# Score products of two heads at once: products over 64 rows in the two halves of the array, decay as bfloat16 rows

## Chip, core and metric

The kernel runs on one core of a Trainium2 chip. TensorE multiplies matrices into PSUM (8 banks), VectorE (DVE), ScalarE (ACT) and GpSimd (POOL) work on tiles in SBUF, SyncE (SP) issues most DMAs. The metric is the device time of one execution in microseconds. An instruction of TensorE takes a stationary operand (the weights, a load of its own in the trace: PEld) and streams a moving one through it, column by column. The array has 128 rows and 128 columns; a product can also occupy half of the rows or half of the columns.

## What is computed

Attention with decay for 4 x 8 heads, 576 positions, head size 64, then two feed-forward stages:

```python
scores = scale * np.matmul(q, k.transpose(0, 1, 3, 2))
cum = np.cumsum(np.log(np.clip(f, 0.0001, 1.0)), axis=-1)
decay = cum[:, :, :, None] - cum[:, :, None, :]
scores = np.where(causal, -1000000000.0, scores + decay)
scores = scores - np.max(scores, axis=-1, keepdims=True)
attn = np.exp(scores)
attn = attn / (np.sum(attn, axis=-1, keepdims=True) + 1e-09)
x = np.matmul(attn, v)          # then [2304, 512]
h = x @ w_in; x = (h / (1 + np.exp(-h))) @ w_out
y = ((x @ w_a) * (x @ w_b)) @ w_out2
```

## The kernel before

Heads are worked on in 16 pairs. A pair's 576 query rows are cut into five blocks (`IB`): four of 128 rows and one of 64. Block 0 needs 128 key columns, block 1 256, block 2 384, block 3 512; block 4 (64 rows of each head, both heads in one tile of 128 partitions) needs 576, in two parts of 288. For each pair, `load_pair` brings q and k, `score` multiplies block by block into PSUM banks named s, takes the row maxima on DVE (into p) and the exponentials on ACT; `inverse` transposes the sums (rs), and spreads their inverses over partitions by a DMA to DRAM and back (invs, rb); `attend` transposes the exponentials on TensorE (t_x, t_y), copies them to th, multiplies by v (pv, in fp32, the two heads in the two column halves of the array), scales by rb on DVE (xf) and writes x in two parts, on ACT and POOL.

Products are made in fp32r, whose operands are rounded, from a high and a low part: high by high, high by low and low by high. Before, this goes into two products over all 128 rows of the array. For each head there is a tile `side` of four slots of 576 columns. In the head's own half of the partitions stand the high parts; the other half holds the low parts, and in slots 2 and 3 a copy of a high part and the decay rows (cum in two parts, and constants). The line `a[:, 0] x a[:, 1]` (L564) gives high by high plus low by high, `a[:, 2] x a[:, 3]` (L566) the rest with the decay. To fill a side, `load_parts` has POOL load q and k with rounding into the head's half (L506), SP copy two slots between or within halves (L508), DVE or POOL subtract the high part from the raw q and k (L511), and SP load the decay rows twice (L516). There are four sides, so two pairs can be prepared at a time. Only pair 0 is different: its heads have tiles `whole` of 66 rows and one product in fp32.

What runs when is decided before the build by `Plan.order`: every piece of work has an engine, a duration, a priority and the buffers that it takes; a simple model of the engines places them in time, and the instructions are issued in that order on each engine. `Tag` stands for a rotating buffer; `SLOTS` has their numbers (before: s 2, t 2, pv 2, mm 2, eight banks in all). The first feed-forward chunk of the first two batches (`first_chunk`, ps and po, 128x288 products) is placed between the attention's work, the decoding of its weights (`plan_decode`) too. After the attention the rest of the feed-forward follows, which is products over 464 columns on TensorE to the end.

At the start `prepare` computes cum on 32 partitions (one for each head), writes its parts to DRAM (dec), and runs 66 idle products; `keep_warm` puts further idle products into TensorE's gaps in the first 40 us of the plan.

Of the kernel before, what the change touches and what calls it, by code (L numbers as in the profile page):

```python
# [55 lines left out]
class Tag:  # L56
# [31 lines left out]
class Plan:  # L88
# [44 lines left out]
    def order(self):  # L133
# [9 lines left out]
        while ready:  # L143
            cands = []
            for op in ready:
                t = 0
                for b in op.bufs:
# [3 lines left out]
                    f = b.tag.free_at() if b.tag.bufs[b.tag.next] is b else None  # L151
# [69 lines left out]
def model_kernel(ctx: ExitStack, tc: tile.TileContext, qk, v, f, w, out):  # L221
# [13 lines left out]
    dec = dram.tile([NH, 2, S], F32, name="dec")  # L235
# [6 lines left out]
    rows_sb = dp.tile([NH, 2, S], F32R, name="rows")  # L242
# [137 lines left out]
    ATT = ("s1", "qkr", "vt", "th", "t3", "t4", "xf", "p", "q", "nm", "sm", "rt", "rb")  # L380
# [14 lines left out]
    def prepare():  # L395
# [16 lines left out]
        def run_up():  # L412
            for n in range(RUN_UP):
# [11 lines left out]
        plan.add("DVE", 369, lambda: nc.vector.tensor_copy(rows_sb[:, 0], cum), ["cum"], [("rows", 0)], pr)  # L425
        plan.add("DVE", 669, lambda: nc.vector.tensor_sub(rows_sb[:, 1], cum, rows_sb[:, 0].bitcast(F32)),
                 ["cum", ("rows", 0)], [("rows", 1)], pr)
        plan.dma(480, 147000, lambda: nc.scalar.dma_start(dec, rows_sb.bitcast(F32)), rows_keys, ["dec"], pr, eng="ACT")
# [4 lines left out]


    sides = [sb.tile([P, 4, S], F32R, name=f"side{n}") for n in range(SLOTS["s1"])]

    def side(h):
        n = len(tags["s1"].bufs) % SLOTS["s1"]
        return Buf(tags["s1"], lambda: sides[n])

    def fill_sides():
        t = sides[-1]
        for n, to in enumerate(sides):
            plan.add("DVE", t_dve(2 * S), lambda to=to, n=n: nc.vector.tensor_scalar(
                half(to, 1 - n % 2)[:, 2:], ident[half_of(1 - n % 2), 0:1].unsqueeze(2).to_broadcast([D, 2, S]), 0.0, None, ALU.mult),
                [("const", 1)], [("side", n)], -7.5 + n)
        for r, i, value in ((4, 3, 1 / SCALE), (2, 2, -1 / SCALE)):
# [5 lines left out]
    def half_of(n):  # L453
        return slice(n * D, (n + 1) * D)

    def half(t, n):
        return t[n * D:(n + 1) * D]
# [450 lines left out]
```

## Time and profile before

| | us |
|---|---|
| three runs | 1088.75, 1089.15, 1089.7 |
| median | 1089.15 |
| profiled execution | 1086.86 |
| its span in the trace | 1085.2 |

The span is the time from the first to the last instruction in the trace; the profiled execution has 1.7 us around it, and is 2.3 us below the median. Durations in the trace are those of one instruction from its start to its modelled end; a stream of products overlaps, so what one adds to a stream is the distance from its start to the next one's start (its pitch).

### The profile page before, as it was taken

How to read it: one execution, taken by the hardware profiler on the slowest of the kernel's cores; microseconds unless marked ns; L12 is line 12 of the kernel's file. 1: busy time of each engine (PE TensorE's matmuls, PEld its weight loads, DVE VectorE, ACT ScalarE, POOL GpSimd, SP SyncE). 2: the span in 40 equal slices, each digit the busy share in tenths (PEclk: the TensorE clock that was granted, in tenths of full speed). 3: DMA queues.
4: the chain of work that ended last, by engine and by line, in shares of the span. 5: the costliest groups of instructions: out<-in, count | busy, mean ns of one | idle time of the engine just before them, and what ended most of it. 6: DMA issues, size and time to landing. Idle time of an engine off the chain costs nothing.

```text
span 1085.2 us, 16074 instructions
## 1 busy us (share of the span) xinstructions
PE 1051.2 (97%) x5625; PEld 914.0 (84%) x5625; DVE 675.7 (62%) x1562; ACT 435.2 (40%) x1082; POOL 354.3 (33%) x416
## 2 busy tenths in 40 slices
PE   8978999999999999999999999999999999999998
PEld 6756677778888889889889898988988988989987
DVE  5778566655998784774845976357366375473323
ACT  3667677775534432332323544343132132231110
POOL 5356445423533330421303774033042051240000
PEclk7989999999999999999999999999999999999999
DMA  5667667732212120110200112012011021010012
GB/s 133 173 187 183 166 173 186 173 94 69 71 58 77 50 78 1 59 59 1 79 1 20 59 43 84 30 40 79 1 59 59 1 78 40 17 62 1 18 53 105
DMA packets 40840, 79.14 MB, mean 73 GB/s; under 512 B 8036, under 2 KB 11252, under 8 KB 40760
## 3 DMA queue, kind: packets, MB, share of 16 engines
q1 hardware_dynamic: 38312, 69.13, 22.0%
q0 software_dynamic: 2400, 8.85, 3.6%
q8 instruction: 44, 0.72, 0.3%
q14 instruction: 36, 0.29, 0.1%
q10 hardware_dynamic: 48, 0.15, 0.0%
HBM read 64.25 MB, written 4.94 MB: 64 GB/s over the span
## 4 chain that ended last, share of the span: by engine, by line
PE 85%; DMA 5%; DVE 4%; ACT 2%; issue 1%; POOL 1%; SPq 1%; DVEq 0%; POOLq 0%; ACTq 0%
PE ps L301 15%; PE ps L302 15%; PE ps L303 15%; PE po L301 10%; PE po L302 10%; PE po L303 10%; PE pv L681 3%; DMA rb<-invs 2%; PE t_x L637 1%; DVE side L511 1%; PE s L564 1%; PE s L562 1%; DVE p L586 1%; PE t_y L637 1%; PE s L566 1%
## 5 line engine op out<-in xcount | busy, mean ns | idle before, releaser
L301 PE MATMUL ps<-x,whi 128*128 128x464 f32 (+1 forms) x760 | 282.6, 372 | 1.7 <-ACT acc L785 1.7
L302 PE MATMUL ps<-x,whi 128*128 128x464 f32 (+1 forms) x760 | 282.6, 372 | 0.0
L303 PE MATMUL ps<-x,wlo 128*128 128x464 f32 (+1 forms) x760 | 282.5, 372 | 0.0
L271 POOL TENSOR_TENSOR d<-d,whi 128x256 f32<-128x256 f32 x124 | 105.7, 860 | 431.3 <-ACT whi L270 431.0
L302 PE MATMUL po<-glo,whi 128*128 128x464 f32 (+1 forms) x520 | 192.4, 370 | 0.0
L303 PE MATMUL po<-ghi,wlo 128*128 128x464 f32 (+1 forms) x520 | 191.9, 369 | 0.0
L301 PE MATMUL po<-ghi,whi 128*128 128x464 f32 (+1 forms) x520 | 190.6, 371 | 0.0
L301 PEld LDWEIGHTS ps<-x,whi 128*128 128x128 f32 x760 | 142.5, 187 | 18.9 <-ACT acc L785 1.9
L303 PEld LDWEIGHTS ps<-x,wlo 128*128 128x128 f32 x760 | 142.4, 187 | 17.2
L302 PEld LDWEIGHTS ps<-x,whi 128*128 128x128 f32 x760 | 142.5, 187 | 17.0
L333 ACT CAST ghi<-g 128x464 fp32r<-128x464 f32 (+1 forms) x130 | 75.0, 577 | 153.5 <-DVE g L332 92.9
L272 POOL TENSOR_TENSOR wlo<-d,d 128x256 fp32r<-128x256 f32 x124 | 100.2, 816 | 35.9 <-DVE d L269 34.6
L263 ACT ACTIVATE d<-d 128x256 f32<-128x256 f32 x124 | 52.9, 433 | 145.6 <-DMA d<-in_w 136.8
L334 DVE TENSOR_TENSOR glo<-g,ghi 128x464 fp32r<-128x464 f32 (+1 forms) x130 | 90.7, 698 | 29.7 <-ACT ghi L333 29.2
L332 DVE TENSOR_TENSOR g<-g,ps 128x464 f32<-128x464 f32 (+1 forms) x60 | 37.8, 631 | 113.3 <-PE ps L303 113.3
L301 PEld LDWEIGHTS po<-ghi,whi 128*128 128x128 f32 x520 | 97.6, 188 | 10.8 <-PE po L303 0.2
L303 PEld LDWEIGHTS po<-ghi,wlo 128*128 128x128 f32 x520 | 97.6, 188 | 10.8
L302 PEld LDWEIGHTS po<-glo,whi 128*128 128x128 f32 x520 | 97.6, 188 | 10.3
L264 DVE TENSOR_SCALAR d<-d 128x256 uint32<-128x256 uint32 x124 | 44.9, 365 | 79.5 <-ACT d L263 78.7
L355 DVE SCALAR_TENSOR_TENSOR acc<-po,acc 128x464 f32<-128x464 f32 (+3 forms) x144 | 75.1, 549 | 26.6 <-PE po L303 26.6
L364 DVE TENSOR_TENSOR acc<-po,acc 128x464 f32<-128x464 f32 (+2 forms) x120 | 63.9, 552 | 26.1 <-PE po L303 25.3
L595 ACT ACTIVATE p<-p,nm 128x512 f32<-128x512 f32 (+3 forms) x128 | 70.8, 557 | 12.4 <-DVE nm L586 12.0
(118 smaller groups left out, 1507.2 us busy)
## 6 DMA issues: line engine op xcount, KB each, us to landing
d<-in_w SPq DMA_DIRECT2D x128, 256.0 KB
side<-in_qk POOLq DMA_DIRECT2D x30, 288.0 KB, 4.9
qk<-in_qk SPq DMA_DIRECT2D x15, 576.0 KB
side<-side SPq DMA_DIRECT2D x60, 144.0 KB
vt<-in_v SPq DMA_DIRECT2D x16, 320.0 KB
rb<-invs SPq DMA_DIRECT2D x32, 128.0 KB
out_t<-acc SPq DMA_DIRECT2D x12, 232.0 KB
d2ghi<-in_w SPq DMA_DIRECT2D x8, 256.0 KB
```

What stands on the lines that cost most here:

```text
L263: nc.scalar.activation(m, high.bitcast(F32), AF.Copy, scale=2.0 ** -112)
L264: nc.vector.tensor_scalar(m.bitcast(U32), m.bitcast(U32), 3, None, ALU.logical_shift_left)
L271: nc.gpsimd.tensor_sub(m, val, hi.bitcast(F32))
L272: nc.gpsimd.tensor_add(lo, m, e)
L301: nc.tensor.matmul(ps, wh, mh, start=start, stop=False)
L302: nc.tensor.matmul(ps, wh, ml, start=False, stop=False)
L303: nc.tensor.matmul(ps, wl, mh, start=False, stop=stop)
L333: nc.scalar.copy(ghi[:, t, :n], g)
L334: nc.vector.tensor_sub(glo[:, t, :n], g, ghi[:, t, :n].bitcast(F32))
L355: nc.vector.scalar_tensor_tensor(a, ps, 0.5, a, ALU.mult, ALU.add)
L364: nc.vector.tensor_add(a, ps, a)
L595: plan.add("ACT", t_act(sum(IB[ib]), 279), lambda b=b, c=c, nj=sum(IB[ib]): nc.scalar.activation(b()[:, :nj], b()[:, :nj], AF.Exp, bias=nm ...
```

## The change

The sides, the loads on POOL's queue, the copies and the subtractions by halves are gone. A pair has one raw tile of q and k (head 0 in partitions 0 to 63, head 1 in 64 to 127, as the array in DRAM has them), one cast of it to the high part (ACT, 128x1152), one subtraction for the low part (POOL or DVE, 128x1152), and a tile `decay` in bfloat16. cum is now in three bfloat16 parts that add up to it exactly; six rows (three parts and constants) stand at partitions 0 and 64 of the decay tile, zeros in the other rows.

A block's scores are four products over 64 rows for each head: decay (bfloat16), high by high, high by low, low by high. The two heads' products alternate; head 0's take rows 0 to 63 of the array, head 1's rows 64 to 127, into two banks. Block 4 has for each of its two parts the decay product and one product in fp32 from the raw tile; its heads use rows and columns 0 to 63, and rows and columns 64 to 127, and write the two halves of one bank. Blocks 1 and 0 form one group (256 and 128 columns in the same two banks).

The buffers change (s 3, pv 1, p 4, vt 2, xf 2, qkr 2), and the planner can place a piece of work that takes two buffers of one kind.

```diff
-    def free_at(self):
+    def free_at(self, ahead=0):
...
-        if len(self.old) < self.slots:
+        n = len(self.old) + ahead - self.slots
+        if n < 0:
             return 0
-        ops = self.old[0].ops
+        ops = self.old[n].ops
...
-    SLOTS = dict(s1=4, qkr=1, vt=1, th=4, t3=1, t4=1, xf=1, s=2, t=2, pv=2, mm=2, g=6, ghi=2, glo=2)
-    SLOTS.update(wh=2, p=3, q=6, nm=2, sm=2, rt=1, rb=1)
+    SLOTS = dict(qkh=2, qkl=2, dt=2, qkr=2, vt=2, th=4, t3=1, t4=1, xf=2, s=3, t=2, pv=1, mm=2, g=6, ghi=2, glo=2)
+    SLOTS.update(wh=2, p=4, q=6, nm=2, sm=2, rt=1, rb=1)
...
-        plan.dma(480, 147000, lambda: nc.scalar.dma_start(dec, rows_sb.bitcast(F32)), rows_keys, ["dec"], pr, eng="ACT")
+        for i, value in enumerate((-1 / SCALE, 1 / SCALE)):
+            plan.add("POOL", 1200, lambda i=i, value=value: nc.gpsimd.memset(rows_sb[:, 3 - 3 * i:6 - 3 * i, i], value), (), [("rows", "const", i)], -8)
+        rest = (ft, one)
+        for n in range(3):
+            src = cum if n == 0 else rest[n - 1]
+            plan.add("DVE", 450, lambda n=n, src=src: nc.vector.tensor_copy(rows_sb[:, n, 0], src), [("c", n), "cum"], [("rows", n)], -8)
+            if n < 2:
+                plan.add("DVE", 750, lambda n=n, src=src: nc.vector.tensor_sub(rest[n], src, rows_sb[:, n, 0]),
+                         [("c", n), ("rows", n), "cum"], [("c", n + 1), ("f", "one")[n]], -8)
...
-            plan.swdge(1040, 8 * D * S, lambda near=near, src=src: nc.gpsimd.dma_start(near()[:, 0:2], src), ["go"], [(s1, "h")], pr + p)
...
+        plan.dma(480, 16 * D * S, lambda: nc.sync.dma_start(raw(), qk[pair]), ["go"], [raw], pr)
         for p in range(2):
...
+            plan.dma(480, 0, lambda p=p: nc.sync.dma_start(dt()[p * D:p * D + 6], dec[2 * pair + p]), ["dec", ("decay", n)], [(dt, p)], pr)
+        plan.add("ACT", t_act(2 * S, 93), lambda: nc.scalar.copy(hi(), raw()), [raw], [(hi, "h")], pr)
+        (e1, d1, f1), two = ((e, d, lambda eng=eng: eng.tensor_sub(lo(), raw(), hi().bitcast(F32)))
+                             for e, d, eng in (("POOL", t_pool(2 * S), nc.gpsimd), ("DVE", t_dve(2 * S) + 300, nc.vector)))
...
+            steps = (4,) if whole else (0, 4) if shared else range(4)
+            todo = [(p, part, n) for part in range(2 if shared else 1) for n in steps for p in range(2)]
...
+                    elif step == 0:
+                        a = half(t["dt"](), p)
+                        nc.tensor.matmul(out, a[:, 0, i], a[:, 1, j], start=True, stop=False)
+                    elif shared:
+                        a = half(t["raw"](), p)
+                        nc.tensor.matmul(out, a[:, 0, i], a[:, 1, j], start=False, stop=True)
+                    else:
+                        a, b = ((t["hi"], t["hi"]), (t["hi"], t["lo"]), (t["lo"], t["hi"]))[step - 1]
+                        nc.tensor.matmul(out, half(a(), p)[:, 0, i], half(b(), p)[:, 1, j], start=False, stop=step == 3)
...
-    GROUPS = ((None, 4),), ((0, 3), (1, 3)), ((0, 2), (1, 2)), ((0, 1), (1, 1)), ((0, 0), (1, 0))
+    GROUPS = (4,), (3,), (2,), (1, 0)
```

The planner places everything anew. On TensorE, before, around the product with v of pair 4 (pv_4; a name is the tile, the pair, and for s the head or None, the block and the part; L757 to L759 are the feed-forward chunk, t_5 transposes):

```order
L637 MATMUL t_5_x0_1308<-ident_58,p_5_1_3_1273 128x2x64
L564 MATMUL s_5_0_0_0_1322<-side0_92 128x128
L681 MATMUL pv_4_1_1327<-th_4_0_1180,vt_4_1116 64x448 x2
L681 MATMUL pv_4_1_1327<-th_4_1_1220,vt_4_1116 64x448 x2
L681 MATMUL pv_4_1_1327<-th_4_2_1229,vt_4_1116 64x320 x2
L681 MATMUL pv_4_1_1327<-th_4_3_1242,vt_4_1116 64x192 x2
L681 MATMUL pv_4_1_1327<-th_4_4_1251,vt_4_1116 64x64 x2
L681 MATMUL pv_4_0_1357<-th_4_2_1229,vt_4_1116 64x128 x2
L637 MATMUL t_5_x1_1362<-ident_58,p_5_None_4_1244 128x128
L566 MATMUL s_5_0_0_0_1322<-side0_92 128x128
L637 MATMUL t_5_x2_1365<-ident_58,p_5_None_4_1244 128x128
```

The single products of a block stand between transposes and pv. After, at the same place (s is now named by pair, block and bank):

```order
L546 MATMUL s_5_1_0_1341<-qkh_5_1024,qkl_5_1034 128x128
L546 MATMUL s_5_1_1_1343<-qkh_5_1024,qkl_5_1034 128x128
L666 MATMUL pv_4_1_1367<-th_4_0_1257,vt_4_1067 64x448 x2
...
L666 MATMUL pv_4_1_1367<-th_4_4_1303,vt_4_1067 64x64 x2
L540 LDWEIGHTS decay1_93
L540 MATMUL s_6_4_0_1395<-decay1_93 64x288
L540 LDWEIGHTS decay1_93
L540 MATMUL s_6_4_0_1395<-decay1_93 64x288
L543 MATMUL s_6_4_0_1395<-qk_6_1057 64x288 x2
...
L543 MATMUL s_6_4_1_1400<-qk_6_1057 64x288 x2
L666 MATMUL pv_4_0_1413<-th_4_2_1277,vt_4_1067 64x128 x2
L622 MATMUL t_5_x0_1421<-ident_58,p_5_None_4_1234 128x128
```

Blocks 1 and 0 of pair 5 come as one run of products before pv_4_1, and block 4 of pair 6 stands between pv_4_1 and pv_4_0, which now use one bank in turn. On SP, before, the DMAs around the broadcast rb of pair 7:

```order
L508 DMA side0_92<-side0_92 64x576 x2
L508 DMA side1_93<-side1_93 64x576 x2
L499 DMA qk_10_1816<-in_qk 128x1152
L610 DMA invs_66<-rt_7_1851 9x128
L616 DMA rb_7_1896<-invs_66 64x512
L494 DMA vt_8_1910<-in_v 128x640
L618 DMA rb_7_1896<-invs_66 64x64
L616 DMA rb_7_1896<-invs_66 64x512
L618 DMA rb_7_1896<-invs_66 64x64
L516 DMA side3_95<-dec_65 2x576 x2
L516 DMA side2_94<-dec_65 2x576 x2
L508 DMA side2_94<-side2_94 64x576 x2
```

After, a pair's whole share of SP's queue (here around rb of pair 4; every later pair reads alike):

```order
L496 DMA decay1_93<-dec_65 6x1152 x2
L494 DMA qk_7_1232<-in_qk 128x1152
L485 DMA vt_5_1242<-in_v 128x640
L595 DMA invs_66<-rt_4_1282 9x128
L601 DMA rb_4_1336<-invs_66 64x512
L603 DMA rb_4_1336<-invs_66 64x64
L601 DMA rb_4_1336<-invs_66 64x512
L603 DMA rb_4_1336<-invs_66 64x64
```

The copies between halves and the dec loads by slots are gone from between the rb DMAs; two decay loads for each pair remain.

## Rows read from the trace of the kernel before

**Rows 1.** The page: busy time, share of the span and instructions of each engine.

```profile
PE 1051.2 (97%) x5625; PEld 914.0 (84%) x5625; DVE 675.7 (62%) x1562; ACT 435.2 (40%) x1082; POOL 354.3 (33%) x416
```

**Rows 2.** Busy time in four stretches: us, engines (instructions), granted clock, DMA share, GB/s.

```profile
40.00:120.00 80.00, 64.47 (x447) 47.26 (x446) 62.19 (x187) 55.68 (x169) 43.12 (x50) 0.94 0.73 181
120.00:200.00 80.00, 73.90 (x523) 57.89 (x523) 50.02 (x168) 57.35 (x168) 40.38 (x40) 0.98 0.69 169
200.00:260.00 60.00, 58.77 (x442) 47.71 (x439) 31.61 (x110) 42.30 (x127) 18.38 (x21) 1.00 0.43 117
...
300.00:400.00 100.00, 100.00 (x478) 89.47 (x478) 85.14 (x184) 39.21 (x87) 38.94 (x48) 1.00 0.20 64
```

**Rows 3.** The chain of work, 0 to 300 us: shares; then start, us, what.

```profile
by line: PE pv L681 12.1%; DMA rb<-invs 8.5%; issue 5.3%; PE t_x L637 4.4%; DVE side L511 3.1%; PE s L564 3.1%; PE s L562 2.9%; DVE p L586 2.9%; PE t_y L637 2.8%; PE s L566 2.5%; ACT p L595 2.1%; DMA side<-in_qk 2.0%; DMA d<-in_w 1.9%; DMA 
...
103.56 6.67 DMA rb<-invs
...
135.07 2.40 DMA rb<-invs
...
159.95 6.05 DMA side<-in_qk
```

**Rows 4.** The subtractions into the sides (L511) in stretches: DVE, POOL busy us.

```profile
220.00:240.00 20.00, 1.83 (x1) 1.38 (x1) 1.00 0.31 91
```

**Rows 5.** Groups by line and shape, 0 to 260 us: busy us, mean ns; idle time before.

```profile
L511 POOL TENSOR_TENSOR side<-qk,side 64x576 fp32r<-64x576 f32 x32 | 49.3, 1541 | 40.8 <-DMA qk<-in_qk 26.7 <-DMA side<-in_qk 10.6 <-DMA side<-dec 1.6
L511 DVE TENSOR_TENSOR side<-qk,side 64x576 fp32r<-64x576 f32 x28 | 31.9, 1139 | 7.0 <-DMA side<-in_qk 4.2 <-DMA qk<-in_qk 2.2
...
L681 PE MATMUL pv<-th,vt 128*64 128x448 f32 x128 | 28.4, 565 | 0.4 <-ACT x L692 0.4
...
L692 ACT CAST x<-xf 128x448 fp32r<-128x448 f32 x16 | 9.0, 564 | 10.6 <-DVE xf L689 10.2 <-POOL d1glo L721 0.5
...
L692 ACT CAST x<-xf 128x128 fp32r<-128x128 f32 x16 | 4.7, 296 | 0.4
```

**Rows 6.** DMAs, 0 to 260 us: the sum; issues by line, KB each, us to landing.

```profile
DMA packets 19188, 40.70 MB, mean 157 GB/s; under 512 B 5636, under 2 KB 5780, under 8 KB 19160
...
side<-in_qk POOLq DMA_DIRECT2D x30, 288.0 KB, 4.9
...
side<-side SPq DMA_DIRECT2D x60, 144.0 KB
```

**Rows 7.** TensorE in order of time, 107.3 to 108.6 us: start, us, line, what.

```profile
107.33 0.39 PE L566 MATMUL s<-side 128*128 128x512 f32 x1
107.56 0.71 PE L637 MATMUL t_y<-ident,p 128*128 128x128 f32 x5
108.05 0.44 PE L564 MATMUL s<-side 128*128 128x384 f32 x1
108.33 0.34 PE L566 MATMUL s<-side 128*128 128x384 f32 x1
108.50 0.38 PE L637 MATMUL t_y<-ident,p 128*128 128x128 f32 x2
```

**Rows 8.** TensorE in order of time: a pair's pv, and what follows it.

```profile
99.89 3.22 PE L681 MATMUL pv<-th,vt 128*64 128x448 f32 x24
103.04 0.33 PE L637 MATMUL t_x<-ident,p_None 128*128 128x128 f32 x1
```

**Rows 9.** TensorE in order of time, 130.2 to 130.6 us: into pv.

```profile
130.24 0.29 PE L564 MATMUL s_None<-side 128*64 128x288 f32 x1
130.37 0.29 PE L566 MATMUL s_None<-side 128*64 128x288 f32 x1
130.59 3.22 PE L681 MATMUL pv<-th,vt 128*64 128x448 f32 x24
```

**Rows 10.** The start, POOL and SP in order of time.

```profile
1.80 1.17 POOL L483 MEMSET whole<- 4x576 f32 x2
...
7.34 2.49 SPq L486 DMA_DIRECT2D whole<-cum  x4
```

More of the change, by code (lines that the diff above doesn't have):

```diff
@@ new lines, in prepare @@
+        rest = (ft, one)
[5 more added lines that the diff above has]
+                         [("c", n), ("rows", n), "cum"], [("c", n + 1), ("f", "one")[n]], -8)
+        plan.add("POOL", 2000, lambda: nc.gpsimd.tensor_copy(rows_sb[:, 3:, 1], rows_sb[:, :3, 0]),
+                 [("rows", n) for n in range(3)], [("rows", "k")], -8)
@@ L430, in model_kernel @@
+        plan.dma(480, 442000, lambda: nc.scalar.dma_start(dec, rows_sb), [("rows", n) for n in (0, 1, 2, "k")] + [("rows", "const", i) for i in range(2)],
+                 ["dec"], pr, eng="ACT")
     wtiles[0] = tuple(w0.tile([P, chunks[0][4]], F32R, name=f"w{n}0") for n in ("hi", "lo"))
     heads = {}
[L435 to L447, printed above, removed]
-            plan.add("POOL", 750, lambda r=r, i=i, value=value: constant(t[:r, i], value), [("const", 1)], [("side", len(sides) - 1)], -7.5)
-        for n, to in enumerate(sides[:-1]):
-            plan.dma(480, 0, lambda to=to, n=n: nc.sync.dma_start(half(to, 1 - n % 2)[:4, 2:].bitcast(F32), t[:4, 2:].bitcast(F32)),
-                     [("side", len(sides) - 1)], [("side", n)], -4 + n)
@@ L453, in half_of, with fill_decays @@
-    def half_of(n):
-        return slice(n * D, (n + 1) * D)
+    decays = [sb.tile([P, 2, S], BF16, name=f"decay{n}") for n in range(SLOTS["dt"])]
     def half(t, n):
         return t[n * D:(n + 1) * D]
-    def constant(t, value):
-        n = t.shape[0]
-        nc.gpsimd.tensor_scalar(t, ident[:n, 0:1].to_broadcast([n, S]), 0.0, value, ALU.mult, ALU.add)
+    def fill_decays():
+        for n, t in enumerate(decays):
+            plan.add("POOL", 1300, lambda t=t: nc.gpsimd.memset(t, 0.0), (), [("decay", n)], -7 + n)
@@ L523, in score @@
         sm, nm = heads["sm", pair], heads["nm", pair]
-        cols = [8 if p is None else 4 * p + ib for p, ib in blocks]
-        parts, tiles = [], []
-        for n, (p, ib) in enumerate(blocks):
-            nj = sum(IB[ib])
-            heads["p", pair, p, ib] = buf(sb, *(("p", [P, S]) if ib > 2 else ("q", [P, 384])), F32, f"p_{pair}_{p}_{ib}")
-            parts += [(n, p, ib, 0, nj)] if nj <= 512 else [(n, p, ib, 0, nj // 2), (n, p, ib, nj // 2, nj // 2)]
-        where = [cols[n] + (j0 > 0) for n, _, _, j0, _ in parts]
@@ new lines, in score @@
+        for p, ib in blocks:
+            heads["p", pair, p, ib] = buf(sb, *(("p", [P, S]) if ib > 2 else ("q", [P, 384])), F32, f"p_{pair}_{p}_{ib}")
+        cols = [8 if p is None else 4 * p + ib for p, ib in blocks]
+        for k, (p, ib, j0, nj, o) in enumerate(parts):
+            s, col = (banks[k], 8 + k) if shared else (banks[p], 4 * p + ib)
+            b = heads["p", pair, p, ib]
+            out, low = (lambda b=b, j0=j0, nj=nj: b()[:, j0:j0 + nj]), (lambda col=col: nm()[:, col:col + 1])
+            if j0 + nj < sum(IB[ib]):
+                plan.add("DVE", t_dve(nj) + 82, lambda out=out, low=low, o=o: nc.vector.tensor_scalar(
+                    out(), o(), -SCALE, None, ALU.mult, ALU.min, accum_out=low()), [s], [(b, j0), (nm, col)], pr + PRIO["max"])
+            else:
+                mk = mask2[:, -nj:] if p is None else maskw[:, -nj:]
+                plan.add("DVE", t_dve(nj) + 82, lambda out=out, low=low, o=o, mk=mk: nc.vector.tensor_tensor_reduce(
+                    out(), o(), mk, -SCALE, 3.0e38, ALU.add, ALU.min, low()), [s, ("const", 3)], [(b, j0), (nm, col)], pr + PRIO["max"])
@@ L591, in score @@
+        if shared:
+            plan.add("DVE", 210, lambda: nc.vector.tensor_scalar(nm()[:, 8:9], nm()[:, 8:9], nm()[:, 9:10], None, ALU.min),
                      [(nm, 9)], [(nm, 8)], pr + PRIO["max"])
@@ L800, in model_kernel @@
     prepare()
-    fill_sides()
+    fill_decays()
     FILL = 4
```

129 lines of the change are left out of this document (50 added, 79 removed).

## The prediction

> **What bounds the kernel now.** I read the page first. TensorE is busy 97% of the span [rows 1], and from about 300 us on it is saturated to the end [rows 2]: there every us that the attention part ends earlier or later goes straight into the total. The change is confined to the attention part, which ends with the last block of x near 255 us. So the question is how much of the time up to there TensorE can't use, and how much work it gets. By stage [rows 2] it is busy 64.47 of 80 us in 40 to 120, 73.90 of 80 in 120 to 200 and 58.77 of 60 in 200 to 260: 81%, 92% and 98%. The mean granted clock is 0.94 and 0.98 in the first two, and they lie at the lower level (1.2 GHz) for about 6.4 us' worth. The other engines are far from full: in 120 to 200 DVE has 50, ACT 57, POOL 40 of 80 us.
>
> Then I read the chain of work in order of time [rows 3], to see what the idle time waits for. In the first 300 us the broadcast of the inverse sums (rb) takes 8.5% (25 us), DVE's and POOL's subtractions into the side tiles and the loads of them several more. One rb took 2.40 us, another 6.67: they queue on SP and on the DMA engines behind the sides' traffic, at a DMA share of 0.73 and 0.69 [rows 2]. At 159.95 the chain waits 6.05 us for the load of one side. After 220 only one subtraction into a side is left on each of DVE and POOL [rows 4]: the sides are done early in just the stage with 98%. I read the idle time of 40 to 200 us as the price of preparing the sides, and the 98% as what TensorE reaches without it.
>
> **The change, part by part.** *Preparation, 15 pairs.* Gone are POOL's 32 subtractions of 1.54 us and DVE's 28 of 1.14 us, 30 loads on POOL's queue (288 KB each), and on SP 60 copies between halves of the sides (144 KB each) and four small dec loads a pair: 17 MB of the 40.7 MB moved in that part [rows 5, 6]. A head pair now has one load, two decay loads, one cast 128x1152 on ACT and one subtraction 128x1152 on DVE (12) or POOL (3). The cast by the slope of the two x casts (0.56 us for 448, 0.30 for 128, so 0.84 ns an element): 1.15 us, 17 us in all on an engine that is idle 30% of 40 to 200: I cost it at nothing. If ACT became the bound, it would cost its 1.15 us a pair. The subtraction is twice the old one's length: 2.3 us by the mean of [rows 5], 27 us where 32 stood, so DVE is even. In the new order it stands directly ahead of xf, for which pv_0 waits: if it runs late, up to 1 us a pair. SP issues 90 DMAs fewer (four copies and four dec loads a pair against two decay loads), and rb no longer stands between copies (the order fences for SP above), so I expect it nearer to 2.40 than to 6.67 us.
>
> *Score products on TensorE.* Before, a pair's scores are 4 products for each of 512, 384, 256 and 128 columns and 8 of 288. Their pitch [rows 7]: 0.23 us for 512 (107.33 to 107.56), 0.17 for 384, so 0.45 ns a column; 0.13 for 288 (130.24 to 130.37 [rows 9]). That is 4 x 1280 x 0.45 ns = 2.30 us and 8 x 0.13 = 1.04. A first product after a transpose pays 0.11 us for its weights (0.28 for the 384 columns at 108.05, 0.17 for the next), in some eight places a pair: 0.9. Together 4.2 us.
>
> After, each block has 4 steps of two 64-row products, one for each head. If the two run side by side, the streams are again 4 x 1280 x 0.45 = 2.30 us; the four steps of 128 columns are held up by the 0.11 us of a weight load instead of 0.06: +0.2. The last block has two parts: a bf16 step of 288 columns (0.13) and a full fp32 step. What that costs the pv rows show: 24 products (6400 columns in all) begin at 99.89 and the next work at 103.04 [rows 8]; two at a time at the 0.11 us per 128 columns of a transpose (0.71 us for five, of which 0.27 is one's length [rows 7]) that is 3200 columns in 2.7 us, 0.85 ns a column and pass; fp32 stands as two passes there. So 2 x 288 x 0.85 = 0.49, and the block costs 2 x (0.13 + 0.49) = 1.24.
>
> Then the array changes shape more often. pv shows the price: 3.15 us less 2.7 leaves 0.45 for three changes (two inside, one at its end), 0.15 each; at its start 0.22 instead of 0.13 [rows 9]. Counted in the program's order there are 64 changes of shape before and 144 after (a group of two heads is one burst; the order fence for TensorE shows pv and the next pair's last block back to back). 80 x 0.15 = 12 us, 0.8 a pair, the first load of a burst included. Sum 2.30 + 0.2 + 1.24 + 0.8 = 4.5 us against 4.2: **+0.3 a pair, +4 us**.
>
> That two products run side by side in halves of the *rows* no row shows. pv shows it for halves of the *columns*: the eight of 448 columns alone last 0.57 us each [rows 5], 4.5 us, and yet all 24 fit in 3.22. The bounds are a full overlap (nothing added) and none: 2.30 + 1.24 = 3.5 us more a pair, 53 us. I take the full overlap, since pv is the nearest row and its loads and streams both overlap.
>
> The Trainium skill ("TensorE: Matmul & The Clock Gate", Measured speedup vs the span model) gives 3.07x for four row tiles of 512 columns; worked out from that page as an estimate, a set side by side takes 1.3 times one product, which would add 0.3 x 3.5 x 15 = 16 us and bring the sum to about zero. No run here shows it so far.
>
> *Start.* Two memsets of rows (32x1728) stand on POOL ahead of those of the whole tiles. By 1.17 us for two of 576 [rows 10] they take 1.8 us each, and the whole tiles must be ready before SP sends cum's rows into them at 7.34. Against that the side constants are gone from DVE. From 0 to +3 us; I take +1. The three-part decay rows add about 2 us on DVE and 2 on POOL (by the same memset), before a use near 30 us: hidden behind pair 0.
>
> *What the idle time gives back.* If 40 to 200 us runs at the 98% of 200 to 260, its 138.4 us of TensorE work take 141.2 instead of 160: -18.8. What is late next is TensorE itself. Sum: -18.8 + 4 + 1 = **-14 us**. The profiled execution took 1086.86 us (span 1085.2), 2.3 below the median of the runs, 1089.15; on the median that gives **1075**. A better clock is not in it: with no fall to 1.2 GHz it would be up to 6.4 us more, and with TensorE at 100% up to 4 more: 1065. If only half of the idle time goes, 1084.
>
> **The rivals.** (a) *Weights one after the other.* The two halves' loads don't overlap: 2 x 0.11 us a step. 512 columns hide that, 384 lack 0.05, 256 lack 0.10, 128 lack 0.11 (on the 0.11 already counted): 4 x 0.26 = 1.04 us a pair, 16 us: 1091. For it: no row shows two loads of 128 columns at once. Against: in pv two loads of 64 columns do not lengthen the pitch.
> (b) *No overlap.* +53 us on a TensorE that is then full: 1128. It ends on the slower side; the point at which it decides is 14/53, a quarter of the overlap lost.
> (c) *One PSUM bank for both halves.* Only in the last block do both heads write one bank. If the two then take turns: +1.24 x 15 = 19 us, 1094. Against: in pv two halves write one bank side by side.
> The Trainium skill ("TensorEngine Tiling (Array Packing)", Gotcha 1: PSUM Pressure) says that different row tiles cannot use the same bank at once; the pv rows don't bear on it, since their two halves share the rows, and so it is this case (c).
> (d) *The idle time wasn't the sides'.* pv has one bank instead of two, so pv_0 and the next rs wait for xf and so for rb; ACT has 17 us more. If two thirds of the 18.8 us stay: -6 + 5, 1088: no change.
>
> **How the numbers follow.** Forecast 0.56 (own range 1063 to 1085), a 0.13, b 0.09, c 0.07, d 0.15. About 0.2% (2.2 us) is what a measurement can tell from no change. Nearly all of the forecast is faster, with a third of a and d, and a quarter of c: 0.66. Slower: b, most of c, half of a, a fifth of d: 0.24. Same: 0.10. The range leaves out b and the ends: 1060 to 1098.
>
> **What would show it.** Right: in the profile after, a head's product starts within some 10 ns of the other's, groups of 512 have a pitch of 0.23 us per step, TensorE in 40 to 200 us is busy 95% or more, rb is near 2.5 us in the chain, and x ends near 240 us. Wrong: a pitch of 0.45 us for two heads (b), 0.22 where 128 columns stream (a), double pitch in the last block alone (c), or a wait of TensorE for xf at pv_0 and a DMA share that fell without TensorE filling up (d).

## The result, and the profile after

The changed kernel takes 1061.63 us, the median of 4 runs (1060.23 to 1062.08), against 1088.95 for the kernel before beside it: a ratio of 0.9753, interval 0.9731 to 0.9775, 27.3 us faster. The forecast was 1075, 14 us faster. The direction held and the time lies in the range of 1060 to 1098, but 1.4 us below the forecast's own range (1063 to 1085): the gain is about twice what the sum said. The profiled execution took 1060.23 us, its span 1058.5.

The busy time of the engines, from the page of the changed kernel, and then the stretches of [rows 2] (us, busy time and instructions of TensorE, its weight loads, DVE, ACT and POOL, granted clock, DMA share, GB/s):

```profile
PE 1043.5 (99%) x5916; PEld 896.8 (85%) x5916; DVE 652.8 (62%) x1539; ACT 453.6 (43%) x1103; POOL 298.7 (28%) x360
```

```profile
40.00:120.00 80.00, 77.80 (x664) 53.90 (x661) 54.40 (x193) 72.05 (x201) 19.56 (x26) 1.00 0.35 115
120.00:200.00 80.00, 79.83 (x699) 56.93 (x697) 47.41 (x177) 71.73 (x203) 13.40 (x18) 1.00 0.27 90
200.00:260.00 60.00, 57.02 (x409) 47.75 (x406) 36.02 (x96) 36.88 (x103) 20.78 (x26) 1.00 0.21 66
```

TensorE is now busy 97% and 99.8% where it had 81% and 92%, at a granted clock of 1.00. The DMA share fell from 0.73 and 0.69 to 0.35 and 0.27. ACT, the second engine, stands at 90% in the first two stretches. (In the third the attention is over after 224 us.)

The chain of work of the changed kernel, 0 to 300 us, for [rows 3] (shares; then start, us, what; all DMA pieces on it ahead of the feed-forward weights):

```profile
by line: PE pv L666 13.6%; PE t_x L622 7.2%; PE s L546 7.1%; PE t_y L622 5.8%; PE s L543 4.0%; PE s L540 3.5%; PE ps L304 3.2%; PE ps L305 3.1%; PE ps L306 3.1%; issue 2.8%; ACT p L580 2.6%; PE po L304 2.3%; PE po L305 2.3%; PE po L306 2.3%
...
25.66 3.70 DMA invs<-rt
...
31.19 2.46 DMA rb<-invs
...
66.57 1.87 DMA invs<-rt
...
70.23 3.51 DMA rb<-invs
```

The broadcast of the inverse sums, rb, had 8.5% of these 300 us; after 74 us it is no longer among the 195 longest pieces of the chain. From there to the end of x at 224 us, some 91% of the chain is TensorE's own work.

The products themselves, in order of time on TensorE (start, us, line, what), one burst of 512 columns for both heads and what follows:

```profile
101.42 0.39 PE L540 MATMUL s<-decay 64*128 64x512 bf16 x2
101.46 0.58 PE L546 MATMUL s<-qkh 64*128 64x512 f32 x2
101.88 0.40 PE L546 MATMUL s<-qkl,qkh 64*128 64x512 f32 x2
102.10 0.41 PE L546 MATMUL s<-qkh,qkl 64*128 64x512 f32 x2
102.44 0.33 PE L622 MATMUL t_x<-ident,p_None 128*128 128x128 f32 x1
```

Each row is both heads' product ("x2"). In the single records the second head's product starts 3 to 18 ns after the first's. Eight products take 1.02 us to the next work; 4 x 0.23 is 0.92, and without overlap it would be 1.84. So the halves of the rows overlap; what the 0.10 beside it is, comes below.

A group of 128 columns and what follows it:

```profile
32.01 0.23 PE L540 MATMUL s<-decay 64*128 64x128 bf16 x2
32.05 0.30 PE L546 MATMUL s<-qkh 64*128 64x128 f32 x2
32.20 0.27 PE L546 MATMUL s<-qkl,qkh 64*128 64x128 f32 x2
32.30 0.28 PE L546 MATMUL s<-qkh,qkl 64*128 64x128 f32 x2
32.51 0.33 PE L622 MATMUL t_x<-ident,p_None 128*128 128x128 f32 x1
```

It takes 0.50 us for four steps, 0.125 each.

The last block, where both heads write halves of one bank (the last columns of pv run into its start):

```profile
98.90 0.31 PE L540 MATMUL s<-decay 64*64 64x288 bf16 x1
...
99.17 0.65 PE L543 MATMUL s<-qk 64*64 64x288 f32 x3
...
99.77 0.65 PE L543 MATMUL s<-qk 64*64 64x288 f32 x3
100.35 0.44 PE L666 MATMUL pv<-th,vt 128*64 128x128 f32 x4
```

From 98.90 to 100.35 it takes 1.45 us; the sum had 1.24 for full overlap, and 2.5 if the heads took turns. In the single records the fp32 products of the two heads come 0.12 us apart, alternating, and each lasts 0.40, so they overlap. (The medians of the 15 pairs for the groups of 512, 384, 256 and 128 columns and the last block are 1.02, 0.79, 0.48, 0.50 and 1.45 us.)

**A ledger.** The x of pair 0 ends at 48.0 us before and 39.6 after (the second cast of its pair on ACT), the x of pair 15 at 255.0 and 224.3. I added up, over all TensorE records between these two ends, the time from each product to the next, by kind; "idle" is where the recorded end of a product lies ahead of the next start. It was done for the experiments too (runs named below), from one profiled execution each. The window holds the scores of 13 to 14 of the 15 pairs on either side: 320 of 360 records before, 600 of 660 after (in fp32 a product of the last block has two records); of transposes it holds 354 and 366.

| us | before | after | b_noprep | f_noprep | f_nodma | b_order | f_traffic | a_banks |
|---|---|---|---|---|---|---|---|---|
| x of pair 0 ends | 48.0 | 39.6 | 49.8 | 48.5 | 48.2 | 45.3 | 42.3 | 40.2 |
| from there to the end of pair 15's | 207.0 | 184.7 | 177.8 | 190.2 | 198.8 | 195.8 | 199.9 | 203.5 |
| TensorE idle in it | 22.3 | 2.4 | 5.6 | 11.0 | 14.7 | 14.8 | 14.0 | 11.2 |
| score products | 58.0 | 57.8 | 55.0 | 55.8 | 56.8 | 56.2 | 59.9 | 59.3 |
| transposes | 37.0 | 44.9 | 32.6 | 34.8 | 37.3 | 36.2 | 45.8 | 47.0 |
| pv | 48.9 | 44.8 | 47.2 | 49.0 | 50.5 | 49.3 | 44.8 | 46.3 |
| feed-forward | 38.3 | 34.4 | 35.7 | 37.4 | 37.3 | 37.6 | 35.0 | 37.9 |

So x ends 30.7 us earlier: 8.4 by the start, 22.3 by the attention, and 19.9 of these are idle time. Of feed-forward products 219 instead of 244 are done by then (3.9 us less in the ledger); they come behind it, and the span is 26.7 us shorter.

**The clock** is a part of it. Before, the granted clock stands at 1.2 GHz from 14.3 us on for 13.65 us, at 58.7 for 6.83, at 116.7 and at 195.2 for 3.41 each. Each of the four falls begins behind or in a gap of TensorE: 1.90 us (from 12.04), 3.93 (from 56.16), 2.45 and 2.34. After, it holds 2.4 GHz from 7 us to the end of the profiled execution (the other three have 0.996 to 0.998 on average). The four stretches that show it at the start (kernel before, then changed kernel; columns as above):

```profile
7.00:14.00 7.00, 5.10 (x78) 4.52 (x78) 2.07 (x4) 0.00 (x0) 4.84 (x9) 1.00 0.66 166
14.00:28.00 14.00, 14.00 (x51) 8.84 (x52) 7.28 (x26) 6.24 (x19) 2.80 (x2) 0.51 0.53 104
```

```profile
7.00:14.00 7.00, 7.00 (x99) 5.83 (x97) 3.98 (x9) 0.62 (x1) 5.55 (x7) 1.00 0.54 173
14.00:28.00 14.00, 13.82 (x133) 10.33 (x132) 10.06 (x37) 11.60 (x32) 8.05 (x6) 1.00 0.46 146
```

Before, TensorE stands idle for 1.9 us of 7 to 14, and this row of the chain of work of the kernel before says on what:

```profile
9.29 4.55 DMA whole<-cum
```

Right after that gap the clock is 0.51. After, there is no gap, and TensorE issues 133 products in 14 to 28 us where it issued 51.

### The profile page after: what moved, and what is told of

The parts are those of the page before. It is cut to its first block, busy times and chain, and to the rows that moved or that the text cites. A ratio compares the mean times of both kernels' runs of the same rounds, so it can differ in the third digit from the quotient of the medians.

```text
span 1058.5 us, 16378 instructions
## 1 busy us (share of the span) xinstructions
PE 1043.5 (99%) x5916; PEld 896.8 (85%) x5916; DVE 652.8 (62%) x1539; ACT 453.6 (43%) x1103; POOL 298.7 (28%) x360
## 4 chain that ended last, share of the span: by engine, by line
PE 92%; DVE 3%; ACT 2%; DMA 2%; issue 1%; SPq 0%; DVEq 0%; ACTq 0%
PE ps L304 15%; PE ps L305 15%; PE ps L306 15%; PE po L304 10%; PE po L305 10%; PE po L306 10%; PE pv L666 4%; PE t_x L622 2%; PE s L546 2%; PE t_y L622 2%; PE s L543 1%; PE s L540 1%; ACT p L580 1%; PE po L742 1%; PE po L743 1%
## 5 line engine op out<-in xcount | busy, mean ns | idle before, releaser
L275 POOL TENSOR_TENSOR wlo<-d,d 128x256 fp32r<-128x256 f32 x124 | 100.2, 816 | 35.6 <-DVE d L272 34.4
L273 ACT CAST whi<-d 128x256 fp32r<-128x256 f32 x124 | 48.6, 403 | 67.3 <-DVE d L268 38.7
```

Of the source, the lines that this page charges most:

```text
L273: nc.scalar.copy(hi, val)
L275: nc.gpsimd.tensor_add(lo, m, e)
```

## The experiments

The theory A at first: the time came from the preparation of the sides, mostly its DMAs, and from the clock at the start. The rivals: it came from the products side by side, from the banks, or from the new plan (the order on each engine, and which of two engines a piece of work gets) that the planner lays when anything is changed; this last one is called theory O in the later runs, and that the work left out was itself the cost, theory W. Ratios are to the kernel before in the same runs; us are worked out from them on 1088.95. What is read from a trace is from one execution of a run.

### The start's clock: b_runup

```diff
-    RUN_UP, WARM = 66, 40000
+    RUN_UP, WARM = 111, 40000
```

> The kernel before with 111 idle products at the start instead of 66, nothing else. They keep TensorE at work over the 1.9 us in which it waits for the second head's decay rows (12.0 to 13.9 us), behind which the clock stood at 1.2 GHz from 14.3 to 28.0 us. Theory A (the start lost time to the clock): the clock holds, pair 0 goes through in about half the time, its x ends near 37 us instead of 44.5, and 5 to 8 us of it reach the end: 1081 to 1084. Rival B (pair 1 waits for its sides anyway): the clock holds, but the end moves by under 2 us: 1087 to 1089. Rival C (the fall has another cause): the clock still falls, no change.

Measured: 1084.07 us, ratio 0.997 (0.9954 to 0.9986), 3.3 us faster. The fall at 14.3 us is gone, and pair 0 ends at 44.1 instead of 48.0. The order of the other engines is the same. So the clock is 3.9 of the 8.4 us at pair 0, and some 3 us of the total, less than the 5 to 8 expected.

### The preparation left out, laid anew: b_noprep, b_nodma, b_nosub

In b_noprep `load_parts` ends at once from pair 3 on, and the scores of these pairs read the sides that pairs 1 and 2 filled:

```diff
+        if pair >= 3:
+            ...
+            return
```

> The kernel before without the preparation of the sides from pair 3 on: no load of q and k, no copies, no subtractions, no decay rows for pairs 3 to 15, whose products read the sides that pairs 1 and 2 left (so their scores are those of other heads); the products on TensorE are all there. Theory A (the idle time of 40 to 200 us was the price of the preparation, as the prediction has it): 18 to 25 us less, 1064 to 1071, the clock stays at 2.4 GHz after 60 us or so, a pair takes about 12.5 us, as in the changed kernel. Rival B (the gain of the change came from the products side by side): under 6 us less, 1083 or more.

In b_nodma only the side loads, the copies and the decay rows are left out, in b_nosub only the subtractions:

```diff
-            plan.swdge(1040, 8 * D * S, ...
+            if pair < 3: plan.swdge(1040, 8 * D * S, ...
-                plan.dma(640, D * S * 4, ...
+                if pair < 3: plan.dma(640, D * S * 4, ...
```

> The kernel before, which from pair 3 on leaves out the DMAs into the sides alone (the rounded loads on POOL's queue, the copies between halves, the decay rows); the load of the raw q and k and the subtractions stay, on what earlier pairs left in the sides. This takes away about the 17 MB that the change takes away. Theory A1 (the queues and the DMA engines held the work up, rb above all): most of what leaving out all preparation gives, 13 us or more less: 1076 or below, rb near 2.5 us in the chain. Theory A2 (DVE's and POOL's subtractions held it up): under 8 us less, 1081 or more.

```diff
-                plan.add(e1, d1, f1, [(s1, "h"), raw], [(s1, k)], pr + p, also=[two])
+                if pair < 3: plan.add(e1, d1, f1, [(s1, "h"), raw], [(s1, k)], pr + p, also=[two])
```

> The kernel before, which from pair 3 on leaves out the subtractions into the sides on DVE and POOL alone (the low parts are then those of earlier pairs); all DMAs stay. Theory A1 (queues and DMA): under 8 us less, 1081 or more. Theory A2 (subtractions): 13 us or more less, 1076 or below. If both this and the run without the DMAs give much, the two are in one chain, in which either is late next when the other goes.

Measured: 1064.09 (0.9785, 0.9764 to 0.9805: 23.4 us), 1074.95 (0.9881, 0.9861 to 0.9902: 13 us) and 1083.79 (0.9958, 0.9939 to 0.9977: 4.6 us). That looked like theory A with the DMAs as the larger part. But the planner had laid all engines anew in these three, and b_start, below, showed that this can't be passed over. One thing holds whatever the plan: b_noprep has the old products and the old two and two banks and yet comes to 1064 us, so neither the products side by side nor the third bank is needed for a gain of this size.

### The loads held at the start, and the plan alone: b_start, b_order

b_start holds the first four side loads until the rows of cum are in the whole tiles: two small copies on POOL read those rows, and the loads come after them.

```diff
+        if pair == 0:
+            for p in range(2):
+                s1 = heads[p]["s1"]
+                plan.add("POOL", 120, lambda ...: nc.gpsimd.tensor_copy(gate[D:D + 2, p], s1()...[D:D + 2, :, 0]),
+                         [(s1, "dec", 0), (s1, "dec", 1)], ["go2"], -7)
...
-                plan.swdge(..., ["go"], [(s1, "h")], pr + p)
+                plan.swdge(..., ["go2" if pair < 3 else "go"], [(s1, "h")], pr + p)
```

> The kernel before with one change: the loads of the sides of pairs 1 and 2 on POOL's queue are held back until the rows of cum are in the whole tiles of pair 0 (two small copies on POOL read them first). Nothing is left out. Theory A (at the start these loads, 4 x 288 KB, delay the rows of cum; TensorE then idles about 2 us and its clock falls to the lower level for 13.65 us): the gap near 12 us shrinks below 1 us, the fall near 14 us goes, pair 0's last x ends at 40 to 44 us instead of 48.0, and the total is 2 to 8 us lower, 1080 to 1086. Rival B (the start is bound by the chain through the decay, whatever else the DMA engines move): the gap stays, pair 0 ends within 1 us of 48.0, 1088 to 1090.

Measured: 1072.14 us, ratio 0.985 (0.9832 to 0.9868), 16 us faster. Neither theory had that. Of what A named only the gap of TensorE shrank, from 1.90 to 0.78 us; the clock still falls at 14.6 us for 13.65 us, and pair 0 ends at 49.7, later than before (in the profiled execution, at 1076.39 us the slowest of the four). The gain lies in the attention, where nothing was changed but the plan. b_order takes this plan and leaves the copies and the hold out: the planner is told of the wait, the chip is not.

```diff
-                plan.add("POOL", 120, lambda ...: nc.gpsimd.tensor_copy(gate...
+                plan.add("POOL", 120, lambda: None, ...
```

> The kernel before with all its instructions, none added and none held back on the chip, but in the order that the planner found for the run with the held loads: it is told that the first four side loads come after the rows of cum, and lays everything behind them anew. Theory O (the order alone moves the kernel by some 15 us): 1070 to 1075, as that run. Rival (it was the held loads themselves): 1085 to 1090, as the kernel before.

Measured: 1072.74 us, ratio 0.9886 (0.9863 to 0.9908), 12.4 us faster, with the work of the kernel before and one idle product more. It is not the order alone: 23 pieces that may run on either of two engines stand on the other one (20 copies of transposes, in both directions between ACT and DVE, and three subtractions, DVE 31 and POOL 29 where it was 28 and 32). Its stretches:

```profile
40.00:120.00 80.00, 70.02 (x476) 52.30 (x474) 60.31 (x186) 57.87 (x170) 48.41 (x51) 0.94 0.75 187
120.00:200.00 80.00, 77.09 (x559) 59.67 (x560) 53.23 (x182) 61.62 (x188) 40.46 (x43) 1.00 0.70 179
```

The DMA share is that of before (0.75 and 0.70), and yet TensorE is busy 70.02 and 77.09 us, not 64.47 and 73.90 [rows 2]. The plan alone takes the idle time from 22.3 to 14.8 us, and pair 0 ends at 45.3 instead of 48.0. Theory O holds.

### The preparation left out, in the order of before: f_noprep, f_nodma

Now the planner sees all the work of before, and from pair 3 on the instructions are dropped where they would be issued:

```diff
-  lambda near=near, src=src: nc.gpsimd.dma_start(near()[:, 0:2], src)
+  lambda near=near, src=src: pair < 3 and nc.gpsimd.dma_start(near()[:, 0:2], src)
```

and likewise the copies and decay rows into the sides (f_nodma), and the subtractions too (f_noprep).

> The kernel before, with its order of instructions on every engine kept exactly, but from pair 3 on the preparation of the sides is left out where it is issued: the loads on POOL's queue, the copies between halves, the decay rows into the sides and the subtractions (the scores of these pairs read what pairs 1 and 2 left there). In the earlier run without preparation the planner had also laid the rest anew. Theory W (the work itself costs): 1062 to 1070 again, TensorE's idle time between the last x of pair 0 and that of pair 15 falls from 22 us to under 8. Theory O (much of the gain is the other order that the planner finds when the work is gone): 1074 to 1084, idle time still 12 us or more.

> As the run without preparation and with the order kept, but the subtractions stay: only the DMAs into the sides (loads, copies, decay rows) are left out from pair 3 on. Theory W: most of that run's gain is here, 1066 to 1076, since rb then lands in some 2.5 us, and the wait for rb all but leaves the chain (it has 8.5% of the first 300 us before). If the subtractions carry it: within 4 us of the kernel before. Theory O: as above, 1078 to 1088.

Measured: 1071.32 us for f_noprep, ratio 0.9869 (0.9852 to 0.9886), 14.3 us; 1078.81 for f_nodma, ratio 0.9933 (0.9914 to 0.9951), 7.3 us (theory O had 1078 to 1088 for it, W 1066 to 1076). The stretches of f_noprep and then of b_noprep, with almost the same work:

```profile
40.00:120.00 80.00, 69.11 (x495) 51.82 (x494) 51.16 (x188) 58.49 (x178) 21.77 (x28) 0.96 0.37 115
120.00:200.00 80.00, 79.41 (x596) 63.80 (x595) 44.58 (x183) 65.75 (x202) 14.20 (x18) 1.00 0.30 93
```

```profile
40.00:120.00 80.00, 73.96 (x567) 57.36 (x566) 57.41 (x209) 63.81 (x195) 24.16 (x31) 1.00 0.24 71
120.00:200.00 80.00, 80.00 (x602) 65.04 (x603) 46.20 (x187) 66.16 (x197) 14.45 (x19) 1.00 0.18 55
```

f_noprep lies between the two theories, and both have a share. The work itself is worth 14 us (half of it the DMAs), and it takes half of the idle time (22.3 to 11.0). The plan that the planner finds once the work is gone is worth some 9 more (23.4 less 14.3; b_noprep also leaves out one load a pair that f_noprep keeps).

### The old traffic put back: a_traffic, f_traffic

a_traffic adds transfers of the old sizes to the changed kernel, into a spare place in memory:

```diff
+        for p in range(2):
+            h = 2 * pair + p
+            plan.swdge(1040, ..., lambda ...: nc.gpsimd.dma_start(spare[h, 0:2], qk[pair, p * D:(p + 1) * D]...
+            for i in range(2):
+                plan.dma(640, ..., lambda ...: nc.sync.dma_start(spare[h, 2 + i], half(raw(), p)[:, i]), ...
```

> The changed kernel with the old DMA traffic put back, but nobody waits for it: for each of the 30 heads of pairs 1 to 15 a load of 295 KB on POOL's queue and two copies of 147 KB on SP's, of the same sizes as those into the sides, all into a spare place in memory. No product, no subtraction, no wait is added. Theory A (what the side transfers cost was their load on the DMA engines and on SP's queue: rb, which stands between them, lands later and x and TensorE wait): 8 to 16 us slower, 1069 to 1078, rb at 4 us or more in the chain, and TensorE under 93% in 40 to 200 us. Rival B (what cost was waiting for the sides themselves): at most 3 us slower, 1061 to 1064. At the start it also shows whether the loads on POOL's queue make the two-byte-row transfers of cum late again: then the clock falls near 14 us and pair 0 ends some 4 to 8 us later.

Measured: 1091.53 us, ratio 1.0035 (1.0022 to 1.0048), some 30 us slower than the changed kernel and outside what either theory had. It isn't the clean run that it was meant to be. Most of the loss is at the start (pair 0 ends at 61.8 instead of 39.6), and there POOL does wait for the transfers, 21.2 us in 12 waits, with its other work queued behind. The order was laid anew as well. It says that such transfers at the start are dear, and no more. f_traffic keeps the order and adds its transfers on SP behind each pair's load, from pair 3 on:

```diff
+            if pair >= 3:
+                for k in range(4):
+                    nc.sync.dma_start(spare[pair, k], qk[pair, :, k % 2])
```

> The changed kernel in its own order, with transfers added that nobody waits for and that wait for nothing: from pair 3 on, behind each pair's load on SP, four transfers of 295 KB from memory to memory, 1.18 MB a pair, about what the sides' loads and copies moved. Unlike the earlier run with added traffic nothing is added at the start and nothing is laid anew. Theory W (traffic on the DMA engines delays rb and with it x and TensorE): 4 to 14 us slower, 1065 to 1076, rb at 3.5 us or more in the chain. If the traffic as such costs nothing in the attention: 1060 to 1064, and then the earlier run's 30 us are the start's and the order's.

Measured: 1079.2 us, ratio 0.9935 (0.9913 to 0.9957), against 0.9753 for the changed kernel: some 20 us slower (0.9935 / 0.9753 = 1.0187), more than the 14 at most that were expected. Its stretches, and what waited on what in 40 to 240 us (total us, times, longest):

```profile
40.00:120.00 80.00, 71.72 (x595) 48.96 (x595) 52.29 (x183) 65.17 (x180) 18.53 (x24) 0.96 0.56 190
120.00:200.00 80.00, 74.52 (x638) 54.03 (x636) 44.19 (x160) 64.87 (x181) 12.56 (x16) 0.98 0.53 181
```

```profile
PE pv L673 <- DVE xf L681: 12.5, 8, 2.7
```

```profile
DVE xf L681 <- DMA rb<-invs: 11.4, 7, 2.7
```

```profile
SPq L608 <- DMA invs<-rt: 45.5, 15, 5.2
```

In the changed kernel the last of these rows reads:

```profile
SPq L601 <- DMA invs<-rt: 16.8, 15, 2.4
```

This is the path of the idle time. SP issues rb only when the 4.5 KB of inverse sums have landed in memory. With the traffic that takes 3.0 us a pair after SP is ready for it, without 1.1. Then rb is late, xf on DVE waits for rb, and pv, which has one bank, waits for xf: 12.5 us of TensorE, of 14.0 idle in the ledger (0.3 us in one wait in the changed kernel). Two falls of the clock, 6.83 us at 38.8 and 3.41 at 178.7, come on top. No wait of SP for the added transfers stands in the trace (three of DVE's rt, 4.2 us, are put down to them), but they are larger in one piece than the old ones (four of 288 KB in a row), so 20 us is no price for the old traffic; f_nodma's 7 us is nearer to that.

### The products in another order: a_serial

```diff
-  todo = [(p, part, n) for part in range(2 if shared else 1) for n in steps for p in range(2)]
+  todo = [(p, part, n) for part in range(2 if shared else 1) for p in range(2) for n in steps]
```

> The changed kernel with the score products of a group in another order: all four steps of one head, then all four of the other, so that two neighbouring products stand in the same half of the rows and cannot lie side by side. The sums and the number of products are the same. Theory A (the two halves of the rows overlap fully, and TensorE bounds the attention): 2.30 us of columns and 1.24 us of the last block are added a pair, 3.5 x 15 = 53 us at most; some of it lies in the 3% of TensorE that stay free, so 1100 to 1118 us. If the halves only overlapped in part already in the changed kernel, the loss would be the smaller: under 25 us, below 1087.

Measured: 1060.57 us, ratio 0.9748 (0.9733 to 0.9763): the same time. It did not take the overlap away. In the program a group of 512 columns now stands like this (the second head's first product carries a wait):

```
906 L540 MATMUL s_6_3_0_1433<-decay1_93 128x512
907 L546 MATMUL s_6_3_0_1433<-qkh_6_1200 128x512
908 L546 MATMUL s_6_3_0_1433<-qkl_6_1209,qkh_6_1200 128x512
909 L546 MATMUL s_6_3_0_1433<-qkh_6_1200,qkl_6_1209 128x512
911 L540 MATMUL s_6_3_1_1438<-decay1_93 128x512 [waits DVE_49]
912 L546 MATMUL s_6_3_1_1438<-qkh_6_1200 128x512
```

and TensorE runs it like this (order of time, columns as above):

```profile
103.01 0.40 PE L540 MATMUL s<-decay 64*128 64x512 bf16 x2
103.05 0.59 PE L546 MATMUL s<-qkh 64*128 64x512 f32 x2
103.46 0.41 PE L546 MATMUL s<-qkl,qkh 64*128 64x512 f32 x2
103.69 0.42 PE L546 MATMUL s<-qkh,qkl 64*128 64x512 f32 x2
104.03 0.33 PE L622 MATMUL t_x<-ident,p_None 128*128 128x128 f32 x1
```

The second head's decay product is the fifth of the group; its record, with the wait, starts 13 ns after the first's and ahead of the first head's second (13 or 14 ns in all 14 groups of 512 columns with the full records). So the worth of the overlap could not be measured by taking it away; that they overlap rests on these rows, on the groups of 512 and 128 columns above and on the ledger, where the score products of 13 to 14 pairs take 57.8 us after and 58.0 before.

### The banks as before: a_banks

```diff
-    SLOTS = dict(..., s=3, t=2, pv=1, ...
+    SLOTS = dict(..., s=2, t=2, pv=2, ...
```

> The changed kernel with the PSUM banks shared out as before: two for the scores and two for pv, not three and one. Theory A (the gain is the preparation that went and the products side by side; the banks only follow from the two-head groups): TensorE has the same work, two banks make the next group of scores wait for the maxima and exponentials of the one before, 0 to 10 us slower: 1062 to 1072. Rival (the order and the third bank carry the gain that I did not forecast, about 13 us): 1075 or more. If pv's single bank costs TensorE anything that counts, this run is faster than 1061.

Measured: 1075.88 us, ratio 0.9891 (0.9874 to 0.9908), some 15 us slower than the changed kernel. Idle time is 11.2 us instead of 2.4, and DVE waits for the score products 29.7 us in 26 waits in 40 to 240 us (12.7 in 15 in the changed kernel). The rival's figure came out. But everything was laid anew here too, so whether the third bank for scores is worth 15 us or the plan that came with it stays open. Within one plan it wasn't tried, and the other buffers that grew (p, vt, xf, qkr) weren't either.

## Why the prediction was right, and short by half

**What bounds the kernel** was read rightly: TensorE's idle time in the attention, at a busy share that has risen to 97% and 99.8% (95% was named). Each us by which x ends earlier came through to the end, less the feed-forward products that are then not yet done (3.9 of 30.7 us; the sum had no term for them).

**The idle time, −18.8.** It fell by 19.9 us. The size is right, the cause only in part, so that it came out this near is in part luck. I had put all of it down to the preparation. With the preparation left out and the order kept, half stays (11.0 us); with the plan alone changed and all the preparation kept, a third goes (22.3 to 14.8). So better plans for the old work existed; that the new kernel's own plan is a good one was not tested, though a_serial, laid slightly otherwise, takes the same time. That the planner lays everything anew, with a model of its own, was in the text before the prediction, but no term or bound of the sum said what a plan by itself can move: 12 us in b_order.

**The start, +1.** This term failed, and with the wrong sign: 8.4 us earlier at pair 0, 9.4 us off, of the 13 us by which the sum is off. I counted POOL's memsets and looked at nothing that waits there. In the trace of before TensorE waits in the start for the DMA of cum's rows, and half the clock follows for 13.65 us; b_runup puts the clock's part at 3.9 us. b_order, with a gap of 0.37 us there, has no fall either; b_start, which has the same plan and the two copies besides, has a gap of 0.78 and the fall. The other 4.5 us lie between the sums of pair 0 and its x. In b_runup, then in the changed kernel (start, us, engine, line, what):

```profile
25.07 0.28 DVE L609 COPY rt<-rs 9x128 f32<-9x128 f32 x1 [0.69 <-PE rs L608]
...
27.09 0.44 SPq L610 DMA_DIRECT2D invs<-rt  x1
...
31.20 0.47 SPq L616 DMA_DIRECT2D rb<-invs  x1
...
39.53 0.62 DVE L689 TENSOR_TENSOR xf<-pv,rb 128x448 f32<-128x448 f32 x1 [1.78 <-DMA rb<-invs]
```

```profile
25.35 0.28 DVE L594 COPY rt<-rs 9x128 f32<-9x128 f32 x1
...
25.66 0.26 SPq L595 DMA_DIRECT2D invs<-rt  x1
...
29.38 0.49 SPq L601 DMA_DIRECT2D rb<-invs  x1
...
34.66 0.61 DVE L674 TENSOR_TENSOR xf<-pv,rb 128x448 f32<-128x448 f32 x1
```

The sums are ready at the same time, but from rt to the first xf it is 14.5 us in b_runup and 9.3 after. In b_runup SP issues four copies and two decay loads into sides (23.88 to 26.99) ahead of invs, and xf waits for rb. By these rows the rest of the start is the sides' traffic on rb's way too; no run takes it away for pair 0 alone.

**The clock, kept out of the sum.** 13.65 us at half the clock lie in the attention of before, none after: up to 6.8 us. The text gave it ("up to 6.4 us more") and left it out. As the falls stand behind or in TensorE's gaps, a forecast that fills the gaps has to take them in.

**The score products, +4.** Full overlap was right, the size of the term was not. In the ledger's window the scores and the transposes around them, into which the changes of shape fall, went from 95.0 to 102.7 us, +7.7; but the 95.0 have clock falls in them. Against b_noprep, which has none there, it is 87.6 to 102.7. The window after holds somewhat more blocks and transposes, so I count by block and by transpose: some +0.85 us a pair and not +0.3, 13 us for 15 pairs and not 4. Of the 0.55 between, 0.2 is the last block (1.45 for 1.24); for the rest the ledger can't say whether the old side was put too high or the new one too low, since a first product's weight load counts with the transpose ahead of it there. My count of 64 changes of shape before leaves out the last block's, between whole and half columns; they show no price in the trace (its products start at 31.72, 31.85, 31.97 and 32.11 us, 0.12 to 0.14 apart, across two such changes). These dearer scores and the clock nearly cancel each other in the result.

**Small terms.** The cast on ACT lasts 1147 ns (1.15 forecast), and ACT is at 90%, not the bound. The subtraction on DVE lasts 1.36 us, not 2.3: 16.3 us for 12, where I had 27 (each is not twice the old one of 1.14 us, as I took it). rb took 2.46 and 3.51 us in the chain and then left it.

**The rivals.** (b) fell by the rows of the burst of 512 columns. (a) fell by the group of 128, which has 0.125 us a step and not 0.22; 512 columns would have hidden it. (c) fell by the last block, 1.45 us and not 2.5. The Trainium skill ("TensorE: Matmul & The Clock Gate", Measured speedup vs the span model) had led to an estimate of 1.3 times one product for a set side by side; the trace has 1.02 us for four steps of 0.23, changes of shape included, so at most 1.1 for these two halves. The Trainium skill's rule on one bank ("TensorEngine Tiling (Array Packing)", Gotcha 1: PSUM Pressure) does not show as a price in time here, where the two heads write different halves of the partitions: 1.45 us. (d) did not come, but its mechanism is real: with rb late, pv on one bank waits for xf 12.5 us in f_traffic.

Put together: about 14 us are the preparation's work, some 9 the plan that goes with its absence (by the pair f_noprep and b_noprep, from pair 3 on and on the old products), and the start gives several more; the dearer scores take some back. The parts overlap, and the shares of the changed kernel's own plan, of its third bank and of its other buffers were not separated.

## What to carry to other kernels

Where a planner lays the instructions, any change is two changes: measure the plan by itself, by keeping it while the work is dropped and by changing it while the work stays, before an edit's effect is put down to its work. A busy engine's gaps cost more than their length where its clock falls behind them (here a gap of 1.90 us and then 13.65 us at 1.2 GHz), so price gap and fall together, at the start too. A small transfer that a chain of waits goes through (here 4.5 KB of sums to memory, then their broadcast) can carry the cost of heavy traffic: look at it, not at the mean share alone.

## What the runs showed of the hardware

- In the trace, products in different halves of the rows do not start strictly in the program's order: in a_serial the fifth product starts 13 ns after the first, ahead of the second, third and fourth, and the time is the same (0.9748 and 0.9753).
- Two products in two halves of the rows start 3 to 18 ns apart and cost little more than one: eight of 512 columns in 1.02 us, where four at the old pitch of 0.23 take 0.92.
- Going into a burst of 64-row products and out of it costs some 0.25 us: in the records of a_serial 0.10 from the last transpose to the first product (0.206 instead of 0.109), 0.10 within the burst, and 0.05 at the next transpose (0.164 instead of 0.109).
- A transfer of 4.5 KB to memory kept SP waiting 1.1 us (16.8 / 15) at DMA shares of 0.27 to 0.35, and 3.0 us (45.5 / 15) at 0.53 to 0.56.
